# A head rearranged: modulation weights by blocks of rows, one block's statistics on ScalarE, fills moved between engines

## The chip, the cores and the metric

The kernel runs on one core of a Trainium2 chip. The metric is the time of one execution on the device in microseconds (us); the numbers given are the median of the runs and their spread. The engines are named as in the profile: PE (TensorE, matrix products; PEld is its loading of weights), DVE (VectorE), ACT (ScalarE), POOL (GpSimd) and SP (SyncE, which here only issues DMAs). ACT issues some DMAs too.

## What is computed

One block with sliding-window attention and a token-mixing MLP, both conditioned by a vector c. S = 2048 tokens, D = 512, 32 heads of 16, window 256, F = 1792; all inputs bfloat16.

```python
mod = silu(c) @ w_mod                      # 6 rows of 512: sa, ca, ga, sb, cb, gb
h = layernorm(x) * (1 + ca) + sa
x = x + ga * attention(h, wqkv, wo)        # causal, keys at most 255 back
h = layernorm(x) * (1 + cb) + sb
u = gelu(einsum('bsd,sf->bdf', layernorm(h), w1) + b1)
x = x + gb * (einsum('bdf,fs->bds', u, w2) + b2).transpose(0, 2, 1)
```

## The kernel before

All is one function. Tokens are cut into 16 blocks of 128 rows (`xres[0]` to `xres[15]`), four blocks make a group, and the features into four chunks of 128 (`dc`). The work has four parts: a head written out by hand (lines 626 to 735), attention over 16 steps (a step is one group of tokens and eight heads), the products with w1, and the products with w2 with the output.

**The head** brings the first group to the first scores. It builds the seeds of the masks (DVE fills, POOL selects), computes silu(c) as `sT` (exp on ACT, `sig` plus one on POOL, reciprocal and product on DVE), the statistics of blocks 0 to 3 (DVE's bn_stats and bn_aggr into `mv1[0]`), from them 1/sqrt(var + eps) as `r1` (POOL adds eps, POOL takes the power -0.5), the normalised blocks `xn1` (DVE), their transposes in PSUM (`pts`, PE), and the shift and scale of the 512 features as columns (`ps_fm`, by PE products of `wmod` with `sT`, one column each). DVE adds 0 or 1 to these (`plus_mod`) into `modFM`, and DVE and ACT write the scaled and shifted transposes to `h1T[0]`, two chunks each. PE then makes the first K and Q (line 720), DVE copies Q twice with alternate heads masked (`QP`, line 727), ACT copies K (`KT`), and the first scores can start. `warm(n)` puts in n filler products of zeros on PE.

For the columns, `fm(b)` takes chunks 2b and 2b + 1 for shift and scale and sums over the four row blocks of `wmod` at once; so it needs all rows of 256 columns, and the weights come in four DMAs of 256 columns and all rows, in runs of 512 bytes. `fm(0)` and `modFM[0]` serve the first two chunks before the transposes of blocks 2 and 3, `fm(1)` the others after them.

V is kept in `Vring[0]` to `Vring[2]`, one for each of three groups, with a column block of ones for each pair of heads, which gives the softmax's sums. The ones are written by ACT in the head (`ones_of`, two operations for each ring place). Zero halves of small copies of V (`VL`, `VU`) are filled by DVE (`zeros_of`), one of them, `VU[1]`, by POOL (line 712).

**What sets the order.** Each engine works off its own instructions in the order in which they were issued; they wait for one another by semaphores. In the head that is the order of the code. From the first scores on a planner (class `Order`) sets it: it takes tasks with an engine, an estimated cost, dependences and a rank, runs a small model of the engines' times and emits the tasks in that order. The ranks come from formulas plus a table, `PLACES`, and `BY` names the engines. The planner does not see the head, and its costs are fixed numbers. In attention ACT takes exp of the scores (line 868, two for each unit of scores) and PE makes scores and products with V; DVE turns the products (`turn`), POOL merges them (`merge`, line 912) and writes `QP` for later steps (line 1048); DVE normalises and transposes the next group (`n1ve`, `n1ng`, `h1T` at line 1155).

SP issues nearly all DMAs in the head in the order of the code: x blocks 0, 1, 3, the four parts of `wmod`, parts of `wqkv`, x blocks 4 to 7; ACT issues c and x block 2. Eight semaphores take turns, so an issue can wait for the landing of the one eight before.

## Time and profile before

| | us |
|---|---|
| median of 3 runs (lowest, highest) | 242.83 (242.56, 243.07) |
| profiled execution | 242.64 |
| its span, first to last instruction | 240.9 |
| PE busy | 234.5 |
| DVE busy | 177.3 |
| ACT busy | 162.1 |
| POOL busy | 96.1 |

The profiled execution is one of its own, and its time is 0.19 us under the median. Rows in order of time have the start in us from the span's start, the length in us, engine, line, operation, what it writes and reads with shapes, and how often (xN: N in a row, with one length for all); square brackets give idle time of the engine ahead of the row and what ended it. Matmul lengths include the pipeline, so neighbouring rows overlap. A row of a tile gives shortest/median/longest in ns. DMA rows give the time from issue to landing.

### The profile page before, as it was taken

To read this page: it belongs to the slowest core of one execution; us is meant where nothing else is said; L and a number is where in the kernel's file an instruction comes from. 1 tells how busy PE (TensorE), PEld (TensorE's weight loads), DVE (VectorE), ACT (ScalarE), POOL (GpSimd) and SP (SyncE) were. 2 spreads that over 40 slices of the span, in tenths; PEclk is the share of its full clock that TensorE was granted. 3 is DMA by queue.
4 is the path that set the end of the run, shared out by engine and by line. 5 is a ranking of instruction groups with operands and counts; after the bars stand their busy time and mean duration, and the time that the engine had idled before them with its cause. 6 is when DMAs were issued, how large, how long until landed. Compare 5 with 4: busy or idle time off the path is not lost.

```text
span 240.9 us, 9884 instructions
## 1 busy us (share of the span) xinstructions
PE 234.5 (97%) x4358; PEld 118.7 (49%) x4358; DVE 177.3 (74%) x421; ACT 162.1 (67%) x188; POOL 96.1 (40%) x149
## 2 busy tenths in 40 slices
PE   7999999999999999999999999999999999999994
PEld 2545555545655554554454455454444444444443
DVE  8799998878999899999356867989964306060644
ACT  7589999999999999999999999900446400000000
POOL 5319775741655466996310113686920000000000
PEclk9999999999999999999999999999999999999999
DMA  5998714063160343210110110069999001111031
GB/s 161 303 345 245 224 32 123 21 169 68 58 181 5 74 113 91 64 35 7 33 38 14 26 38 3 3 199 393 413 405 407 18 0 46 44 44 44 24 111 44
DMA packets 26151, 28.09 MB, mean 117 GB/s; under 512 B 10488, under 2 KB 23292, under 8 KB 26108
## 3 DMA queue, kind: packets, MB, share of 16 engines
q1 hardware_dynamic: 25956, 27.33, 36.0%
q8 instruction: 34, 0.56, 1.0%
q10 hardware_dynamic: 152, 0.13, 0.2%
q14 instruction: 9, 0.07, 0.1%
HBM read 22.55 MB, written 2.10 MB: 102 GB/s over the span
## 4 chain that ended last, share of the span: by engine, by line
PE 74%; DVE 19%; POOL 2%; issue 2%; ACT 2%; DVEq 0%; ACTq 0%; POOLq 0%
PE bk L606 18%; PE pss L1451 15%; PE bk L890 7%; PE pss L606 6%; PE bk L610 6%; PE pss L847 6%; DVE stats L599 5%; PE bk L1451 5%; PE bk L624 3%; DVE x L1255 2%; DVE t L899 2%; PE pss L859 2%; PE pss L819 2%; PE pss L828 1%; DVE QR L740 1%
## 5 line engine op out<-in xcount | busy, mean ns | idle before, releaser
L868 ACT ACTIVATE et<-pss 128x1024 bf16<-128x1024 f32 x152 | 141.7, 1050 | 1.5 <-PE pss L859 1.3
L1451 PEld LDWEIGHTS <-w2r 128*128 128x128 bf16 x238 | 23.1, 98 | 25.5
L912 POOL TENSOR_TENSOR merge<-t,zr 128x512 bf16<-128x512 f32 x16 | 16.9, 1058 | 32.3 <-DVE zr L908 32.2
L1460 DVE SCALAR_TENSOR_TENSOR o<-pss,bFM,bc_gb 128x512 bf16<-128x512 f32 (+2 forms) x13 | 8.8, 705 | 27.9 <-PE pss L1451 27.9
L1451 PE MATMUL pss<-guT,w2r 128*128 128x512 bf16 (+2 forms) x130 | 28.4, 363 | 0.0
L899 DVE STREAM_TRANSPOSE t<-bk 128x512 f32<-128x512 f32 x32 | 22.6, 706 | 7.2 <-PE bk L890 7.0
L847 PE MATMUL pss<-QP,KT 32*128 32x64 bf16 (+2 forms) x672 | 24.2, 236 | 0.7 <-DVE QP L727 0.3
L606 PE MATMUL bk<-h1T,wqkv 128*128 128x512 bf16 x80 | 21.0, 381 | 0.0
L1048 POOL TENSOR_SCALAR QP<-QR,mask_par 128x512 bf16<-128x512 bf16 x22 | 15.1, 694 | 14.8 <-PE pss L859 9.7
L606 PE MATMUL bk<-hb,w1a 128*128 128x512 bf16 x82 | 20.6, 380 | 0.2 <-DVE t L899 0.2
L606 PE MATMUL pss<-hb,w1b 128*128 128x512 bf16 x80 | 20.1, 379 | 0.1
L847 PEld LDWEIGHTS <-KT 32*128 32x128 bf16 x672 | 11.2, 92 | 17.7 <-issue 15.1
L890 PE MATMUL bk<-et,V 128*32 128x256 bf16 (+2 forms) x704 | 19.0, 240 | 0.7 <-DVE t L899 0.4
L599 DVE BATCH_NORM_STATS2 stats<-x 128x6 f32<-128x512 bf16 x28 | 18.8, 673 | 0.2
L890 PEld LDWEIGHTS <-V 128*32 128x32 bf16 x704 | 15.2, 97 | 7.2 <-issue 2.7
L606 PEld LDWEIGHTS <-w1b 128*128 128x128 bf16 x112 | 10.9, 98 | 13.7 <-issue 0.5
L859 PE MATMUL pss<-mask_q,mask_k 32*128 32x256 bf16 x240 | 17.5, 268 | 0.0
L606 PE MATMUL bk<-wod,OT 128*128 128x512 bf16 x54 | 13.9, 381 | 0.0
L606 PEld LDWEIGHTS <-w1a 128*128 128x128 bf16 x90 | 7.9, 98 | 10.3 <-issue 2.5
L606 PE MATMUL bk<-wqkv,h1T 128*128 128x512 bf16 x47 | 12.8, 381 | 0.0
L1255 DVE TENSOR_TENSOR x<-bk,x 128x512 bf16<-128x512 f32 x16 | 10.8, 674 | 2.8 <-PE bk L606 2.8
L921 DVE STREAM_TRANSPOSE OT<-merge 128x512 bf16<-128x512 bf16 x16 | 11.2, 700 | 2.0 <-POOL merge L912 1.8
(145 smaller groups left out, 396.5 us busy)
## 6 DMA issues: line engine op xcount, KB each, us to landing
w2r<-in_B_w_dram SPq DMA_DIRECT2D x14, 512.0 KB, 10.6
w1a<-in_B_w_dram SPq DMA_DIRECT2D x16, 224.0 KB, 3.7
w1b<-in_B_w_dram SPq DMA_DIRECT2D x8, 448.0 KB, 6.7
wmod<-in_w_mod_dram SPq DMA_DIRECT2D x4, 512.0 KB, 6.9
x<-in_A_x_dram SPq DMA_DIRECT2D x15, 128.0 KB, 5.4
out_dram<-otile SPq DMA_DIRECT2D x15, 128.0 KB, 1.8
VL<-V SPq DMA_DIRECT2D x15, 96.0 KB, 2.3
wmod<-in_w_mod_dram SPq DMA_DIRECT2D x4, 256.0 KB, 4.3
```

Of the source, the lines that this page charges most:

```text
L599: nc.vector.bn_stats(out=stats[:], in_=src)
L606: nc.tensor.matmul(out[:], lhsT=lhsT, rhs=rhs, start=start, stop=stop, skip_group_check=True)
L610: nc.tensor.matmul(out[cols, :], lhsT=lhsT[:, cols], rhs=rhs, start=start, stop=stop, tile_position=(0, 32 * j), skip_group_check=True,)
L847: mm(pss[j // 2][:, j % 2, c0 : c0 + nq], lhsT=keys(4 * tg + kb)[rows[j], :], rhs=QP[s][rows[j], par, q0 : q0 + nq], start=n == 0, stop=False,
L859: mm(o, lhsT=mask_k[rows[j], 0:P], rhs=rhs, start=False, stop=True, tile_position=(32 * j, 0), skip_group_check=True,)
L868: nc.scalar.activation(out=et[:], in_=held.pop(("pss", u, a))[:], func=ACT.Exp, scale=SCORE_SCALE)
L890: nc.tensor.matmul(po[32 * j : 32 * j + 32, q0 : q0 + nq], lhsT=v(j), rhs=held["et", s, k, j // 2][:, j % 2, c0 : c0 + nq], start=n == 0, ...
L899: nc.vector.transpose(out=held["t2", s][:, par, :], in_=psum.pop(("po", s, par))[:])
L912: nc.gpsimd.tensor_tensor(out=m[:].rearrange("p (b a d) -> p a b d", a=2, d=DH), in0=t2v(s, 0, DH, DH), in1=held["zr", s][:].to_broadcast( ...
L1048: engine[by(f"Qp{s}.{par}", "POOL")].tensor_scalar(out=QP[s][:, par, :], in0=QR[s][:], scalar1=mask_par[:, par : par + 1], scalar2=0.0, op ...
L1255: nc.vector.tensor_tensor(out=xres[tb][:], in0=pa[:], in1=xres[tb][:], op=ALU.add)
L1451: nc.tensor.matmul(py[:, lo:hi], lhsT=w2r[:, fc, tb * P : (tb + 1) * P], rhs=guT[fc][:, lo:hi], start=fc == made[0], stop=fc == made[-1], ...
```

## The change

*Weights by rows.* The shift and scale weights come in four DMAs of one row block each (128 rows, 1024 columns, runs of 2 KB); the first is issued by ACT, the others by SP. `fm(k)` now adds row block k to all eight columns, in one PSUM tile and one `modFM` of eight columns; its four calls are interleaved with the transposes, which now go block by block.

*Statistics.* Those of block 2 are made by ACT: the mean as an accumulated sum, a small step for its negative, and the variance as an accumulated square; both throw their wide output into `h1T[0]`, which is written for good later. DVE does blocks 0, 1 and 3, and adds eps for both pairs. POOL keeps the two powers, and its copy of `sT` (`sT_rep`) moves ahead of them.

*Fills.* ACT's fills of ones shrink from six to three and move behind the masks. Half of `Vring[1]` goes to DVE ahead of `modFM`. `Vring[2]` is filled by POOL behind the merge of step 0, in attention, in a task whose planned cost stays as it was. `VU[1]` goes from POOL to DVE. All selects of POOL come in one piece. The fillers on PE go from eleven to six ahead of the mask rows, with two ahead of `fm(0)` and two behind `fm(3)` instead of one, two and one.

*Ranks.* Two terms of -1e4 for steps done by ACT are dropped; the order of the rows that follow the head is otherwise unchanged on each engine, apart from the new fill on POOL.

DVE in the head before, from block 1's aggregate to the last of the four normalised blocks (x_64 to x_67 are blocks 0 to 3):

```order
L646 BN_AGGR mv_0_230<-stats 128x2
L643 BN_STATS stats<-x_66 128x6
L645 RECIPROCAL sig<-sig 128x4
L646 BN_AGGR mv_0_230<-stats 128x2
L648 TENSOR_TENSOR sT<-pss,sig 128x4
L643 BN_STATS stats<-x_67 128x6
L646 BN_AGGR mv_0_230<-stats 128x2
L683 TENSOR_SCALAR xn_332<-x_64,mv_0_230,r_293 128x512
L683 TENSOR_SCALAR xn_338<-x_65,mv_0_230,r_293 128x512
L534 MEMSET VU_214 64x384
L683 TENSOR_SCALAR xn_363<-x_66,mv_0_230,r_307 128x512
L683 TENSOR_SCALAR xn_369<-x_67,mv_0_230,r_307 128x512
```

The same place in the changed kernel (r_ve is variance plus eps):

```order
L598 BN_AGGR mv_0_229<-stats 128x2
L652 TENSOR_SCALAR r_ve<-mv_0_229 128x2
L666 RECIPROCAL sig<-sig 128x4
L667 TENSOR_TENSOR sT<-pss,sig 128x4
L597 BN_STATS stats<-x_67 128x6
L598 BN_AGGR mv_0_229<-stats 128x2
L652 TENSOR_SCALAR r_ve<-mv_0_229 128x2
L532 MEMSET VU_213 64x384
L699 TENSOR_SCALAR xn_335<-x_64,mv_0_229,r_298 128x512
L699 TENSOR_SCALAR xn_341<-x_65,mv_0_229,r_298 128x512
L699 TENSOR_SCALAR xn_355<-x_66,mv_0_229,r_305 128x512
L699 TENSOR_SCALAR xn_369<-x_67,mv_0_229,r_305 128x512
```

Block 2's statistics are gone, two small additions have come in, and the fill of VU stands ahead of all four normalised blocks. POOL in the head, before, from `sig` to the copy of `sT`:

```order
L634 TENSOR_SCALAR sig<-sig 128x4
L487 AFFINE_SELECT seed_182<-seed_182 16x64
L553 TENSOR_SCALAR r_ve<-mv_0_230 128x2
L555 TENSOR_TENSOR r_293<-r_ve,mhalf 128x2
L487 AFFINE_SELECT seed_181<-seed_181 16x64
L487 AFFINE_SELECT seed_182<-seed_182 16x64
L553 TENSOR_SCALAR r_ve<-mv_0_230 128x2
L555 TENSOR_TENSOR r_307<-r_ve,mhalf 128x2
L712 MEMSET VU_215 64x768
L746 COPY sT_rep<-sT 128x128
```

And now:

```order
L632 TENSOR_SCALAR sig<-sig 128x4
L485 AFFINE_SELECT seed_181<-seed_181 16x64
L485 AFFINE_SELECT seed_180<-seed_180 16x64
L485 AFFINE_SELECT seed_181<-seed_181 16x64
L668 COPY sT_rep<-sT 128x128
L659 TENSOR_TENSOR r_298<-r_ve,mhalf 128x2
L659 TENSOR_TENSOR r_305<-r_ve,mhalf 128x2
```

Both additions and the fill are gone, and the copy has moved ahead of the first power. POOL in attention around the merge of step 0, before:

```order
L1048 TENSOR_SCALAR QP<-QR,mask_par 128x512 x2
L912 TENSOR_TENSOR merge<-t_729,zr 128x2x16x16
L1048 TENSOR_SCALAR QP<-QR,mask_par 128x512 x2
L582 TENSOR_TENSOR n1r<-n1ve,mhalf 128x4
L584 TENSOR_TENSOR n1sh<-n1ng,n1r 128x4
```

And now:

```order
L1068 TENSOR_SCALAR QP<-QR,mask_par 128x512 x2
L927 TENSOR_TENSOR merge<-t_720,zr 128x2x16x16
L937 MEMSET V 128x64x16
L1068 TENSOR_SCALAR QP<-QR,mask_par 128x512 x2
L580 TENSOR_TENSOR n1r<-n1ve,mhalf 128x4
L582 TENSOR_TENSOR n1sh<-n1ng,n1r 128x4
```

The fill stands between the merge and the two QP of step 2. The diff, cut to its core:

```diff
-    for b in range(2):
-        for v in range(2):
-            cols = slice(v * D + 2 * P * b, v * D + 2 * P * b + 2 * P)
-            dma.dma_start(out=wmod[:, :, cols], in_=w_mod_v[:, :, cols])
+    for k in range(ND):
+        (dma if k else nc.scalar).dma_start(out=wmod[:, k, 0 : 2 * D], in_=w_mod_v[:, k, 0 : 2 * D])
...
-        run_selects(1)
+        run_selects(3)
...
-        for n in range(3):
-            ones_of(n)
...
+        def stats_by_act(tl):
+            neg = small.tile([P, 1], DT.float32, name="neg")
+            junk, mean = h1T[0][:, 0, :], mv[:, tl, 0:1]
+            nc.scalar.activation(out=junk, in_=xres[tl][:], func=ACT.Identity, scale=1.0 / D, accum_out=mean)
+            nc.scalar.activation(out=neg[:], in_=mean, func=ACT.Copy, scale=-root)
+            nc.scalar.activation(
+                out=junk, in_=xres[tl][:], func=ACT.Square, scale=root, bias=neg[:], accum_out=mv[:, tl, 1:2]
+            )
...
+        stats_by_act(2)
+        for tl in (0, 1, 3):
+            stats_of(xres[tl][:], mv[:, tl, :])
+            if tl == 1:
+                ve[0] = eps_of(0)
+                nc.vector.reciprocal(out=sig[:], in_=sig[:])
+                nc.vector.tensor_tensor(out=sT[:], in0=cT[:], in1=sig[:], op=ALU.mult)
+                nc.gpsimd.tensor_copy(out=sT_rep[:], in_=sT[:].unsqueeze(2).to_broadcast([P, ND, 32]))
+                power(0)
+        ve[1] = eps_of(1)
+        power(1)
+        zeros_of(0, True)
+        warm(6)
-        warm(11)
...
+        ones_of(0)
+        ones_of(1, 1)
...
+        warm(2)
+        fm(0)
+        turn_x(0)
+        turn_x(1)
+        fm(1)
+        turn_x(2)
+        fm(2)
+        turn_x(3)
+        fm(3)
+        warm(2)
+        nc.vector.memset(Vring[1][:, 2:4, :, DH : 2 * DH], 1.0)
+        nc.vector.tensor_tensor(out=modFM[:], in0=ps_fm[:], in1=plus_mod[:], op=ALU.add)
...
-        nc.gpsimd.memset(VU[1][0:64, :, :, :], 0.0)
+        zeros_of(1, True)
...
+        def more_ones(s):
+            merge(s)
+            if s == 0:
+                nc.gpsimd.memset(Vring[2][:, :, :, DH : 2 * DH], 1.0)
...
-                f"merge{s}", "POOL", 1.035, lambda s=s: merge(s), port=True, deps=[f"recip{s}"], take=[("m", s)],
+                f"merge{s}", "POOL", 1.035, lambda s=s: more_ones(s), port=True, deps=[f"recip{s}"], take=[("m", s)],
...
-                rank=rank + BEHIND["p2"] - (1e4 if first_eng == "ACT" else 0.0),
+                rank=rank + BEHIND["p2"],
```

## Prediction

> **What bounds the kernel now.** I read the page's span and chain first, then busy time by stage, then the first 13 us in order of time on DVE, POOL, PE and ACT, then the stretch from 26 to 32 us, where the only edit outside the head sits. Page, then stages (columns: stretch, PE, PEld, DVE, ACT, POOL busy us, clock, DMA share, GB/s):

> ```profile
> span 240.9 us, 9884 instructions
> PE 74%; DVE 19%; POOL 2%; issue 2%; ACT 2%; DVEq 0%; ACTq 0%; POOLq 0%
> ...
> 20.00:31.00 11.00, 10.34 (x289) 6.11 (x291) 10.79 (x25) 11.00 (x14) 9.06 (x14) 1.00 0.65 196
> ...
> 40.00:145.00 105.00, 104.16 (x2892) 54.97 (x2893) 88.27 (x183) 104.80 (x114) 51.80 (x63) 1.00 0.25 64
> ```

> The chain runs mostly over PE, but in attention ACT too is busy without a break: 11.00 of 11 us and 104.80 of 105. So the attention stage ends when the first exp starts, plus ACT's fixed work, plus what ACT idles. Two things can move the end: the start of the first exp, and new idle time in front of a later one. The head in order of time (start, length, engine, line):

> ```profile
> 3.78 0.26 POOL L634 TENSOR_SCALAR sig<-sig 128x4 f32<-128x4 f32 x1
> 4.65 0.18 DVE L646 BATCH_NORM_AGGREGATE mv<-stats 128x2 f32<-128x6 f32 x1
> 5.33 0.16 DVE L645 RECIPROCAL sig<-sig 128x4 f32<-128x4 f32 x1
> 5.67 0.68 DVE L643 BATCH_NORM_STATS2 stats<-x 128x6 f32<-128x512 bf16 x1
> 6.39 0.18 DVE L646 BATCH_NORM_AGGREGATE mv<-stats 128x2 f32<-128x6 f32 x1
> 6.50 0.70 DVE L683 TENSOR_SCALAR xn<-x,mv,r 128x512 bf16<-128x512 bf16 x2
> 6.67 0.30 POOL L553 TENSOR_SCALAR r_ve<-mv 128x2 f32<-128x2 f32 x1 [0.28 <-DVE mv L646]
> 7.05 0.72 POOL L555 TENSOR_TENSOR r<-r_ve,mhalf 128x2 f32<-128x2 f32 x1
> 7.22 0.38 DVE L534 MEMSET VU<- 64x384 uint32 x1
> 7.72 0.73 POOL L712 MEMSET VU<- 64x768 bf16 x1
> 7.80 1.12 DVE L683 TENSOR_SCALAR xn<-x,mv,r 128x512 bf16<-128x512 bf16 x2 [0.21 <-POOL r L555]
> 8.99 0.61 PE L688 MATMUL pss<-identity,xn 128*128 128x128 bf16 x8
> 9.43 0.54 PE L671 MATMUL bk<-sT,wmod 128*128 128x1 bf16 x16
> 9.63 1.45 ACT L706 ACTIVATE h1T<-pss,modFM 128x512 bf16<-128x512 bf16 x2 [1.16 <-PE pss L688]
> 10.04 0.15 DVE L701 TENSOR_TENSOR modFM<-bk,plus_mod 128x4 f32<-128x4 f32 x1
> 10.23 0.55 DVE L702 TENSOR_SCALAR h1T<-pss,modFM 128x512 bf16<-128x512 bf16 x1
> 10.69 0.34 DVE L510 TENSOR_REDUCE mask_par<-identity 128x1 f32<-128x64 bf16 x2
> 11.16 0.38 DVE L534 MEMSET VL<- 64x384 uint32 x1
> 11.84 1.14 DVE L727 TENSOR_SCALAR QP<-bk,mask_par 128x384 bf16<-128x384 f32 x2 [0.30 <-PE bk L720]
> 13.05 3.78 ACT L868 ACTIVATE et<-pss 128x1024 bf16<-128x1024 f32 x4 [0.88 <-PE pss L859]
> ```

> Read backwards: the first exp (13.05) waits for scores, these for QP (11.84), QP for the first products, these for the fourth piece of h1T, which ACT ends at 9.63 + 1.45 = 11.08. ACT waited for the transposes, and they for the last xn (7.80 + 1.12 = 8.92), which came after four statistics on DVE and an add and a power on POOL. The wait before 7.80 names POOL's r.

> **The change, part by part.** *Statistics and epsilon.* Block 2's statistics leave DVE, and POOL's add of epsilon becomes a DVE operation. DVE's series from the end of block 1's aggregate (4.65 + 0.18 = 4.83): epsilon 4.86, reciprocal 4.93, sT 5.12 (it needs the reciprocal, 0.16), block 3's statistics 5.20 to 5.88 (0.68), aggregate to 6.10, second epsilon 6.13 to 6.29, the fill of VU 6.20 to 6.58. The reciprocal comes 0.4 us sooner than at 5.33; sig is ready at 4.04. ACT now issues one weight DMA before its table load, which delays sig by an issue, about 0.5 us (rows below), to 4.54 at most: still ahead.

> POOL: the sT copy now stands ahead of the first power. sT ends at 5.28, the copy about 0.33 later at 5.69 (my estimate from the 0.30 of the small POOL row at 6.67), first power to 6.42, second 6.42 to 7.15. Before, the second ended at 7.77. The first is later than before, but VU's fill holds DVE until 6.58 anyway. A power does not hold DVE: VU's fill at 7.22 took 0.38 inside one, as the fill at 11.16 did beside nothing.

> *xn.* Now four in a row: two from 6.55 to 7.25 (0.70 a pair), two from 7.22 to 7.92. Before, the second pair took 1.12, since POOL filled half of VU beside it:

> ```profile
> L683 DVE TENSOR_SCALAR xn<-x,mv,r x4: 378/399/800, 6.5 to 8.5; 128x512 bf16<-128x512 bf16 x4
> ```

> One of the four took 800 ns instead of some 380. That fill moves to DVE, so 0.42 us goes. The last xn ends at 7.92 instead of 8.92: 1.00 us sooner.

> *Scale and shift.* Part of this is given back. Before, half of modFM was ready early and ACT started with the transposes; now one modFM stands behind all 32 weight products. After the last xn: four transposes start from 7.99, 0.056 apart (8 in 0.61, one lasts 0.22), then eight products 0.025 apart with a tail of 0.16 (16 in 0.54): end 8.61. modFM 8.68 to 8.83; ACT's two pieces 8.91 to 10.36 (1.45) instead of 11.08. So 0.72 of the 1.00 is left. From ACT's end to QP it was 11.84 - 11.08 = 0.76: QP at 11.12. DVE must be there too: two h1T from 8.87, 0.46 apart, masks at 9.79, fills of VL 10.26 and VU about 10.64 to 11.02. It just fits (0.10 spare). The fill of V ahead of modFM lies in the 0.7 us in which DVE waits for PE.

> *Statistics on ACT.* Three operations, none seen with an accumulated sum. Nearest rows: a 512-wide fill below, the 1024-wide exp of the 13.05 row above (four in 3.78, 0.95 each).

> ```profile
> 1.38 0.36 ACTq L436 DMA_DIRECT2D x<-in_A_x_dram  x1
> ...
> x<-in_A_x_dram ACTq DMA_DIRECT2D x1, 128.0 KB, 2.6
> ...
> L539 ACT ACTIVATE V<-zero 128x512 bf16<-128x512 bf16 x6 | 3.2, 617 | 0.0
> ```

> Block 2 lands at 1.38 + 2.6 = 3.98. At 0.62 for each wide one and some 0.4 for the one-column step between them with its waits it ends near 5.7, ahead of the second epsilon (6.13). I take that, since the size is the fill's. At 0.95 each, with waits of 0.6, it ends near 6.5 and pushes the second power by 0.4; sooner than the epsilon it gains nothing. Behind it stand four small mask copies (estimate by size: 1 us) and three fills of ones (3.2 / 6 each, 1.6 us), to 8.3, before h1T at 8.91.

> *Wider packets.* Issues and landings of the four weight loads:

> ```profile
> 2.18 2.09 SPq L440 DMA_DIRECT2D wmod<-in_w_mod_dram  x4
> ...
> DMA to landing us min/median/max: 4.1/4.3/4.5
> ```

> The last was issued near 3.75 and landed near 8.3; its products started at 9.43. Nothing waited for it, so wider packets alone are worth nothing here. They only must not be late: SP's third issue falls near 3.2, with 4.5 it lands at 7.7, needed at 8.2; at half a microsecond more it would cost that excess.

> *The fill in attention.* POOL fills Vring[2] behind the first merge.

> ```profile
> 26.10 1.06 POOL L912 TENSOR_TENSOR merge<-t,zr 128x512 bf16<-128x512 f32 x1 [1.11 <-DVE zr L908]
> 27.62 1.36 POOL L1048 TENSOR_SCALAR QP<-QR,mask_par 128x512 bf16<-128x512 bf16 x2 [0.46 <-DVE QR L740]
> ...
> 28.41 0.60 DVE L575 TENSOR_SCALAR n1ng<-n1mv 128x4 f32<-128x4 f32 x1
> 28.91 0.98 DVE L1155 TENSOR_SCALAR h1T<-bk,modFM 128x512 bf16<-128x512 bf16 x2
> ...
> 29.09 0.40 PE L837 MATMUL pss<-QP,KT 32*128 32x512 bf16 x4
> 29.95 1.05 PE L610 MATMUL bk<-wqkv,h1T 128*32 128x512 bf16 x16 [0.35 <-DVE h1T L1155]
> ...
> 25.86 5.77 ACT L868 ACTIVATE et<-pss 128x1024 bf16<-128x1024 f32 x6
> 32.03 1.02 ACT L868 ACTIVATE et<-pss 128x1024 bf16<-128x1024 f32 x1 [0.40 <-PE pss L859]
> ```

> Its 1024 elements at the 730 ns for 768 of the POOL fill above make 0.97 us, starting at 27.16. The gap there is 0.46, so the QP pair goes from 27.62 to 28.13 (+0.51) and the scores that need it from 29.09 to 29.60. PE has 0.35 us of waiting right behind them and ACT 0.40 before 32.03, so about 0.16 is left. If the fill packs its elements (half the price) the gap covers it: 0. If it takes 1.35 (twice a QP of 512), the pair is 0.87 late and 0.5 is lost. I take 0.15, by the only POOL fill in the trace of its size.

> Two edits cost nothing: the ranks of the LayerNorm steps on ACT leave every engine's row order there as it was, and the wider plus_mod fill is one small fill near 1 us, ahead of any need.

> **Sum.** -0.72 + 0.15 = -0.57 us. The profiled execution took 242.64 (span 240.9); its start and end outside the span don't change, so 242.07 there, and against the median of the runs, 242.83, 242.26. A measurement tells about 0.2%, 0.49 us, from no change; -0.57 is just beyond it.

> [...] DVE's 28.41 row took 0.60 for four elements: it ended when POOL's second QP did (28.98). With both QPs 0.51 later, the two tiny DVE operations meet them at another phase. If both slip between the two QPs, h1T stays at 28.91; if the second waits for the later QP, h1T goes to 29.4 and PE's wait at 29.95 grows by 0.5.
> [...]

> **Rivals.** (1) *The fill eats the gain*: h1T 0.5 later as above, or the fill at 1.35; -0.72 + 0.5 gives 242.6, no change. For it: the 28.41 row. Against: the same row's neighbour slipped through. (2) *The head gains little*: ACT's sums at the upper price, or the last weights late by 0.4; -0.72 + 0.4 + 0.15 gives 242.66, no change. For it: ACT's accumulation is unseen. Against: 0.2 us spare at the likely price. (3) *Slower: PE is still at its slow rate when the first products come.* Five filler products go from the start, and PE's rate rises only after a stretch of work:

> ```profile
> 2.33 4.85 PE L624 MATMUL bk<-zero 128*128 128x512 bf16 x11
> ...
> 8.15 0.59 PE L624 MATMUL bk<-zero 128*128 128x512 bf16 x2
> ```

> Eleven in 4.85 are 0.43 apart, two in 0.59 are 0.21 apart. Eight products of 384 columns at the slow 0.32 from 9.45 would end near 12.2 instead of 11.1, and the eight small ones behind them lose 0.4: together +1.5, net 243.7. It decides only if the slow rate lasts beyond about 11 us. Against: with fillers, mask rows and the first weights PE is still busy almost without a gap to 6.5, and the trace turned fast by 8.15.
> [...]

> **How the numbers follow.** Forecast 0.57 (own range 241.95 to 242.55: the head 0.55 to 0.85, the fill 0 to 0.2; some four fifths of it beyond the bound, one fifth inside). Fill eats the gain 0.20, all within 0.2%. Head gains little 0.11, within. Slow PE 0.12, nearly all slower. Faster 0.46, within 0.43, slower 0.11. The range goes from 241.95 to 243.0: it leaves out the slow PE's upper part and some of the lower tail.

> **What would show it.** Right: first QP near 11.1 and first exp near 12.35; four xn of 0.4 without a long one; the second power ending near 7.15; weights landed before PE reaches them; the POOL fill of about 1 us near 26.5, and ACT's idle before the exp at 32.03 larger by some 0.15 in all. Wrong: an epsilon that waits for ACT, filler products still 0.43 apart at 8 us, or PE waiting 0.8 us for h1T near 29.

## The result, and the profile after

| | before | after |
|---|---|---|
| median of the runs beside each other, us | 242.93 | 245.83 |
| lowest, highest (6 runs each) | 242.56, 243.39 | 244.91, 248.07 |
| ratio after / before, 95% interval | | 1.0131 [1.0085, 1.0177] |
| profiled execution, its span | 242.64, 240.9 | 245.19, 243.5 |

The change made the kernel slower by 2.9 us; the forecast was 0.57 faster, range 241.95 to 243.0. The page of after, span and busy times:

```profile
span 243.5 us, 9875 instructions
PE 235.1 (97%) x4353; PEld 119.0 (49%) x4353; DVE 176.8 (73%) x422; ACT 162.6 (67%) x190; POOL 95.9 (39%) x147
```

Busy times are those of before within 1 us (PE 234.5 there); what grew is idle time and slow time. Against before, the first exp starts 0.40 later (13.45 against 13.05), the exps from 26 us on 0.74, from 32 us 1.43, from 40 us 1.73, and the end comes 2.6 later. So the loss comes in steps, and only the first is in the head. The last lies behind attention, whose last exp is 1.6 late: near 165 us PE waits 0.8 us for the weights w1b to land, which it did not do before. The rows of the two pages, before and after (busy us, mean ns, then idle us ahead and what ended it):

```profile
L606 PE MATMUL pss<-hb,w1b 128*128 128x512 bf16 x80 | 20.1, 379 | 0.1
```

```profile
L604 PE MATMUL pss<-hb,w1b 128*128 128x512 bf16 x80 | 20.0, 380 | 0.8 <-DMA w1b<-in_B_w_dram 0.8
```

The head of after in order of time, PE:

```profile
2.50 2.74 PE L622 MATMUL bk<-zero 128*128 128x512 bf16 x6
5.18 0.71 PE L676 MATMUL bk<-seed,spread 16*128 16x320 bf16 x2
5.82 1.03 PE L622 MATMUL bk<-zero 128*128 128x512 bf16 x2
...
8.77 0.40 PE L691 MATMUL pss<-sT,wmod 128*128 128x1 bf16 x8
9.03 0.59 PE L704 MATMUL pss<-identity,xn 128*128 128x128 bf16 x4
9.41 0.40 PE L691 MATMUL pss<-sT,wmod 128*128 128x1 bf16 x8
9.67 1.01 PE L622 MATMUL bk<-zero 128*128 128x512 bf16 x2
```

The last two fillers start 0.38 apart: PE is still at its slow rate at 9.67, where before had two in 0.59 (0.21 apart) at 8.15. The trace's record of the granted clock has the full rate from 7.02 us on in before and from 10.56 on in after. DVE, POOL and ACT of after in the head:

```profile
5.74 0.19 ACT L644 ACTIVATION_READ_ACCUMULATOR h1T<-x,neg 128x1 f32 x1
6.48 0.17 DVE L652 TENSOR_SCALAR r_ve<-mv 128x2 f32<-128x2 f32 x1
6.73 1.13 POOL L659 TENSOR_TENSOR r<-r_ve,mhalf 128x2 f32<-128x2 f32 x1 [0.29 <-DVE r_ve L652]
6.97 0.54 DVE L699 TENSOR_SCALAR xn<-x,mv,r 128x512 bf16<-128x512 bf16 x2
7.90 0.74 DVE L699 TENSOR_SCALAR xn<-x,mv,r 128x512 bf16<-128x512 bf16 x2 [0.39 <-POOL r L659]
9.85 0.17 DVE L719 TENSOR_TENSOR modFM<-pss,plus_mod 128x8 f32<-128x8 f32 x1 [0.67 <-PE pss L691]
12.24 1.14 DVE L745 TENSOR_SCALAR QP<-bk,mask_par 128x384 bf16<-128x384 f32 x2
13.45 1.02 ACT L883 ACTIVATE et<-pss 128x1024 bf16<-128x1024 f32 x1 [0.89 <-PE pss L874]
```

The last xn ends at 8.64, 0.28 sooner than before, but modFM starts at 9.85 and the first QP at 12.24, 0.40 later than before. In attention, PE of after, and the exp behind it on ACT:

```profile
26.10 0.25 PE L834 MATMUL pss<-QP,KT 32*64 32x128 bf16 x4 [0.18 <-issue]
...
32.57 0.27 PE L905 MATMUL bk<-et,VL 128*32 128x64 bf16 x12 [0.90 <-issue]
...
33.46 1.02 ACT L883 ACTIVATE et<-pss 128x1024 bf16<-128x1024 f32 x1 [1.08 <-PE pss L874]
```

At 26.10 and 32.57 PE stops inside a series of products and waits for nothing that the profile shows ("issue"). The exp behind the second stop waits 1.08 where before it waited 0.40 (at 32.03). The place of these stops has a pattern. The page of after lists a queue of instruction packets, q8, with 34 of them and 0.56 MB, so 16 KB each. A row of PE is one product or one load of weights; there are 8706 of them (4353 each), 256 for each packet. Counted in order of start, the two stops come at rows 702 and 958, exactly 256 apart, and PE goes on 1.3 us (26.10) and 1.4 us (32.57) after a packet of this queue has landed (24.81, 31.13). Of the 33 packets behind the first, 31 start between 0.9 us ahead of and 4.0 us behind PE's arrival at row 446, 702, 958 and so on. So I read them as PE's program, which comes in pieces of 256 rows while it runs, with borders at rows 190, 446, 702, 958 and so on (an estimate from these counts). The changed kernel has five fillers less, ten rows, so each border lies ten rows later in the work. Two theories came from this: *the clock* (with five fillers less PE stays slow, or falls back) and *the code pieces* (a piece's packet waits in the load burst of 23 to 30 us, and PE arrives first). The third was that the moved fills and loads carry the loss by themselves. (Times of the clock and of packets are given from the span's start here; the expectations on record count both from 0.31 us before it.)

### The profile page after: what moved, and what is told of

It reads as the page before. It is cut to its first block, busy times and chain, and to the rows that moved or that the text cites. A ratio compares the mean times of both kernels' runs of the same rounds, so it can differ in the third digit from the quotient of the medians.

```text
span 243.5 us, 9875 instructions
## 1 busy us (share of the span) xinstructions
PE 235.1 (97%) x4353; PEld 119.0 (49%) x4353; DVE 176.8 (73%) x422; ACT 162.6 (67%) x190; POOL 95.9 (39%) x147
## 4 chain that ended last, share of the span: by engine, by line
PE 70%; DVE 17%; DMA 5%; issue 2%; POOL 2%; SPq 1%; ACT 1%; DVEq 0%; ACTq 0%
PE bk L604 18%; PE pss L1471 15%; PE bk L905 7%; PE pss L604 6%; PE pss L862 6%; PE bk L608 6%; PE bk L1471 5%; DVE stats L597 5%; DMA w1b<-in_B_w_dram 4%; PE pss L834 2%; PE pss L874 2%; DVE t L914 2%; DMA x<-in_A_x_dram 2%; PE pss L843 1%; DVE QR L758 1%
## 5 line engine op out<-in xcount | busy, mean ns | idle before, releaser
L927 POOL TENSOR_TENSOR merge<-t,zr 128x512 bf16<-128x512 f32 x16 | 16.9, 1056 | 32.6 <-DVE zr L923 32.5
L597 DVE BATCH_NORM_STATS2 stats<-x 128x6 f32<-128x512 bf16 x31 | 21.0, 677 | 0.5 <-DMA x<-in_A_x_dram 0.2
## 6 DMA issues: line engine op xcount, KB each, us to landing
x<-in_A_x_dram SPq DMA_DIRECT2D x15, 128.0 KB, 5.2
out_dram<-otile SPq DMA_DIRECT2D x15, 128.0 KB, 1.8
```

Of the source, the lines that this page charges most:

```text
L597: nc.vector.bn_stats(out=stats[:], in_=src)
L927: nc.gpsimd.tensor_tensor(out=m[:].rearrange("p (b a d) -> p a b d", a=2, d=DH), in0=t2v(s, 0, DH, DH), in1=held["zr", s][:].to_broadcast( ...
```

## The experiments

| kernel | median us (lowest, highest; runs) | ratio to before, 95% |
|---|---|---|
| e1: after, 11 fillers | 243.0 (242.61, 244.46; 12) | 1.0006 [0.9986, 1.0026] |
| e2: after, 6 and 5 tiny | 244.55 (242.16, 245.97; 9) | 1.0048 [1.0018, 1.0078] |
| e3: before, 6 fillers | 245.22 (244.24, 245.42; 6) | 1.0080 [1.0055, 1.0104] |
| e4: before, 6 and 5 tiny | 243.75 (242.64, 246.3; 12) | 1.0020 [1.0001, 1.0040] |
| e5: e1 with the head reordered | 242.95 (242.16, 247.88; 12) | 0.9991 [0.9972, 1.0010] |
| e6: e1, fill back on ACT | 243.85 (243.37, 244.66; 8) | 1.0036 [1.0020, 1.0052] |
| e7: e1, wod load later | 243.08 (242.52, 243.43; 12) | 0.9995 [0.9980, 1.0010] |
| e8: e1, two tiny on ACT | 243.68 (243.2, 244.76; 12) | 1.0030 [1.0015, 1.0045] |
| e9: after, wod load later | 245.24 (243.24, 246.71; 11) | 1.0079 [1.0047, 1.0111] |
| e10: e5, wod load later | 242.8 (242.25, 243.86; 12) | 0.9985 [0.9967, 1.0003] |
| e11: before, wod load later | 242.71 (242.6, 244.27; 12) | 0.9990 [0.9972, 1.0008] |
| e12: e8, wod load later | 243.17 (242.39, 243.75; 12) | 0.9996 [0.9978, 1.0014] |

The kernel before took 243.08 beside e1 to e4, 243.14 beside e5 to e8 and 242.88 beside e9 to e12. A filler has 512 columns and a tiny one four; the two tiny operations on ACT in e8 have one.

### e1 to e4: the fillers, their rows and their work

e1, and e2 in place of it; e3 and e4 are the same edits of before, whose call was `warm(11)`:

```diff
-        warm(6)
+        warm(11)                      # e1
+        warm(6)                       # e2
+        warm(5, cols=4)
```

> The changed kernel with eleven fillers on PE ahead of the mask rows again instead of six; all else as changed. Clock theory (six fillers leave PE's clock to come late or fall back): the clock is up near 7 to 8 us, the time returns to about 243 (242.3 to 243.8). Code theory (PE's instruction stream is ten rows shorter, so it reaches the ends of its 256-row pieces before the next piece is there, as at 26.1 and 32.6 us in the changed kernel): ten rows are back, so also about 243 to 243.8, with no stall at those rows. Third theory (the loss is made by the moved fills and loads): 245.5 or more as before this edit.

> The changed kernel with its six fillers and five more of only four columns behind them: ten rows more on PE, but next to no work. Clock theory: no help, 245 to 247, the clock up at 10 us or later or falling back. Code theory: about 243 to 244, no stall of PE inside a group of products near 26 and 32 us. Third theory: 245.5 or more.

> The kernel before with six fillers instead of eleven, nothing else: PE idles between about 5 and 6.5 us and its stream is ten rows shorter. Clock theory: 244 to 246, with the clock late in some executions. Code theory: 243.7 to 244.5, stalls of PE near 25 and 31 us. Third theory: 242.9, no change.

> The kernel before with six fillers and five of four columns: the rows are as many as before, only PE's work is less. Clock theory: 244 to 246 as with six alone. Code theory: 242.9, no change. Third theory: 242.9.

Five fillers put back take away the whole loss (245.83 to 243.0, the time of before), and five taken from before cost it 2.1 (243.08 to 245.22). So everything else in the change together is worth nothing that can be measured (the forecast gain of 0.57 would be a ratio of 0.9977, below e1's interval), and the theory of moved fills and loads falls. The five tiny products, which bring the rows back and hardly any work, recover about half: 1.28 in after, 1.47 in before. The clock shows in the stages of e2 (stretch, then PE, PEld, DVE, ACT, POOL busy, granted clock, DMA share, GB/s):

```profile
2.70:6.11 3.41, 3.41 (x14) 1.24 (x13) 2.69 (x9) 2.92 (x9) 2.45 (x11) 1.00 0.97 297
6.11:9.52 3.41, 2.25 (x47) 1.84 (x46) 2.82 (x9) 2.18 (x7) 1.47 (x2) 1.00 1.09 323
9.52:12.94 3.42, 3.37 (x19) 1.31 (x17) 2.19 (x8) 1.45 (x2) 0.00 (x0) 0.50 1.10 339
```

The record of the clock begins with its first rise, at 6.11 here (the column reads 1.00 ahead of it too, though the fillers there are 0.43 apart). PE then worked 2.25 of the next 3.41, and its rate fell back to half for one stretch, 9.52 to 12.94, just when the first products of Q and K came; the first exp started at 14.48. Within a run the changes of the clock lie a whole number of 3.41 us apart (e2: 6.11, 9.52, 12.94; after: 10.56 and 242.67, 68 of them); the expectations call this stretch the window. Its phase, and with it the first rise, differs from trace to trace: with the same eleven fillers the rise lies between 4.97 (e7) and 7.27 us (e6), and it came at 4.11 in e5.

How often the rate falls back is seen in the mean granted clock of each run: with six fillers in the second place (after, e2, e3, e4, e9) it is 0.984 to 0.993 in 22 of 44 runs, with ten or eleven (the other kernels and before in their company) in 1 of 183 (e5's 247.88). In e9 the seven such runs have a median of 245.44 and the other four 243.59; in e2 and e4 the difference is 0.95 and 0.53, and in after and e3 there is none that way. But this mean counts the time ahead of the first rise as full, so it misses a rate that comes late: e3's profiled run has a mean of 1.000, and its full rate came only at 12.67. In the three traces in which the slow rate met the first products of Q and K (e2, e3, e9), the first exp starts 1.42 to 1.54 later than in before. These products in before and in e3:

```profile
10.24 1.55 PE L720 MATMUL bk<-h1T,wqkv 128*128 128x384 bf16 x8
```

```profile
11.10 2.23 PE L720 MATMUL bk<-h1T,wqkv 128*128 128x384 bf16 x8
```

How many runs got the full rate late, and whether the tiny products change that number, is not shown.

### e5: the head's order

> The changed kernel with 17 fillers again, and the order in the head mended: fm(0) to fm(3) stand ahead of the transposes of blocks 2 and 3, ACT makes two fills ahead of the mask rows and one on either side of the copy of K, and DVE fills nothing ahead of modFM. Theory (PE's order, and not the normalised blocks, carried the head of the changed kernel with its fillers back, where modFM started at 9.81 and the first exp at 13.41): modFM near 8.5, first QP near 11.1, first exp near 12.3, so 1.1 us sooner; the time is 243.0 - 1.1 = 241.9, or up to 242.5 where PE, being sooner, meets more of its late code pieces (rows 702 and 958). Rival (the head is held by DVE or by weights of Q and K that have not landed): first exp at 13.2 or later and 242.9 to 243.2. Rival (the clock): the last four fillers come 1 us sooner, a window of 3.4 us falls thin, and products near 9.5 run at the slow rate: 244 or more in some runs.

```diff
+        ones_of(0)              # ahead of the mask rows
...
-        warm(2); fm(0); turn_x(0); turn_x(1); fm(1)
-        turn_x(2); fm(2); turn_x(3); fm(3); warm(2)
+        warm(1); fm(0); fm(1); turn_x(0); fm(2); turn_x(1); fm(3)
+        turn_x(2); turn_x(3); warm(4)
-        nc.vector.memset(Vring[1][:, 2:4, :, DH : 2 * DH], 1.0)
```

(There are ten fillers ahead of the mask rows; the two halves of `Vring[1]` are filled by ACT on either side of its copy of K.) DVE and ACT of e5:

```profile
8.44 0.17 DVE L717 TENSOR_TENSOR modFM<-pss,plus_mod 128x8 f32<-128x8 f32 x1
...
11.07 1.14 DVE L744 TENSOR_SCALAR QP<-bk,mask_par 128x384 bf16<-128x384 f32 x2
...
12.29 1.94 ACT L883 ACTIVATE et<-pss 128x1024 bf16<-128x1024 f32 x2 [0.37 <-PE pss L874]
```

These are the values that the forecast had for the changed kernel (QP 11.12, first exp 12.35). But this profile also had the full rate from 4.11 us, the earliest of all. Four profiles with the same 11 fillers and nearly the same head show what the phase alone does: the first exp starts at 12.51, 13.04, 13.41 and 13.47 where the full rate starts at 4.97 (e7), 6.15 (e8), 7.06 (e1) and 7.27 (e6), 0.42 us for each us. Carried on to 4.11 that line gives 12.15 (an estimate), sooner than e5's 12.29. So the theory's 1.1 us is not shown, and the median, 242.95 against 243.0, speaks for the rival.

### e6 and e8: the fill in attention, and ACT's own code pieces

> The changed kernel with 11 fillers, and its POOL fill of Vring[2] in attention taken back to two fills of ACT in the head, in the time in which ACT waits for the mask rows. Forecast's term (the fill costs 0.15, bounds 0 to 0.5): 243.0 - 0.15 = 242.85. Theory that the fill is free since n1ng slips ahead of the second QP: the same start of the exps near 32 us, to 0.1. ACT's code pieces (128 rows each, a border at row 62): two rows more move the border from between a semaphore wait and its exp, near 40 us, to between two exps, so the extra 0.3 at 39.6 goes: 242.7. If instead that 0.3 comes from what PE or DVE do there, it stays.

> The changed kernel with 11 fillers and two one-column operations more on ACT in the head, where it waits for the mask rows; they do no work. Theory (ACT's code comes in pieces of 128 rows; crossing a border costs 0.3 where it falls between a semaphore wait and its exp, and is hidden behind the exp in front where it falls between two exps): ACT's border moves by two rows, and the exp that started 1.23 after the one before it, near 40.2, starts 0.92 after it; 242.7. Rival (PE's scores or a buffer hold that exp): 1.23 stays, 243.0.

```diff
+        ones_of(2)              # e6, ahead of the mask rows
-            if s == 0:
-                nc.gpsimd.memset(Vring[2][:, :, :, DH : 2 * DH], 1.0)
...
+        for n in range(2):      # e8, at the same place
+            nc.scalar.activation(out=junk1[:], in_=zero[:, 0:1], func=ACT.Copy)
```

The exps that the forecast had in mind (32.03 in before) can't be compared between e6 and e1, because PE stops at row 958 ahead of them in both. Ahead of that stop the exps start alike, near 29 us at 29.10 without the fill (e6, head 0.06 later) and at 29.11 with it (e1). e7 below has the fill and no such stop, and there this exp, the first of the row below, waits 0.22, where in before it waited 0.40, so the fill costs nothing:

```profile
31.30 11.34 ACT L883 ACTIVATE et<-pss 128x1024 bf16<-128x1024 f32 x12 [0.22 <-PE pss L874]
```

The step of 0.3 near 40 us is ACT's: in all kernels made from after with 309 rows on ACT one exp starts late, right behind the event on which it waited, at ACT's row 63. ACT in e1, the exp at 40.21 and the two before it, and the same place in e8:

```profile
38.08 2.00 ACT L883 ACTIVATE et<-pss 128x1024 bf16<-128x1024 f32 x2
...
40.21 1.02 ACT L883 ACTIVATE et<-pss 128x1024 bf16<-128x1024 f32 x1
```

```profile
38.71 2.02 ACT L886 ACTIVATE et<-pss 128x1024 bf16<-128x1024 f32 x2
```

In e1 the second exp of the first row starts at 38.98 and the next 1.23 behind it; in e8, with two rows more on ACT, the two in the row start 0.92 apart, and so do those of e6. So that step hangs on the number of rows ahead of it, as a border between two pieces of ACT's program would have it. That a piece has 128 rows is an estimate (on the page of after the other instruction queue, q14, has 9 packets and 0.07 MB, so 8 KB each, half of the 16 KB that go with 256 rows of PE), since one border alone was seen. It is worth nothing at the end, though: in the median e6 is 0.85 and e8 0.68 slower than e1, not faster. Their profiles have longer stops at row 958 (0.74, 0.53, against 0.43 in e1) and waits for w1b near 165 to 170 us (0.35, 1.31), which e1's lacks; whether that is the doing of the edits or the spread of one execution stays open.

### e7, e9, e11, e12: the load burst

> The changed kernel with 11 fillers; the load of wod (512 KB), which SP issued near 23 us, is issued behind the V copies of the step after, near 34 us, still before its use at 41. Nothing else moves. Theory (PE's code pieces queue behind the load burst): the packet for row 958 lands near 29 instead of 30.5, PE does not stop at row 958 (0.53 before), and the exps from 33 us on come 0.4 to 0.5 sooner: 242.5. A stall at row 1214 or 1470 may take its place, 0.3 at most, since those had 1.7 spare. Rival (the stall is the wait for something else, data or a buffer): 0.53 stays at that row and the time is 243.0.

> The changed kernel as it is, with its six fillers, and the load of wod behind the V copies near 34 us. Theory (of the 2.9 that the change cost, about half is PE's code pieces that land too late behind the load burst, half the slow rate in the head): the idle time of PE at rows 702 and 958 (0.46 and 1.17 in the profile of the changed kernel) goes, the head stays as it is: 245.8 - 1.3 = 244.5, ratio near 1.006. Rival (the slow rate carries all, and those stalls are a mark of a late head): 245.8 as before, ratio 1.012. Rival (the pieces carry all): 243.0, ratio 1.000.

> The kernel before, with the load of wod later and nothing else. Theory: its rows 702 and 958 had 0.1 to 0.2 to spare in the one profile, so the later load gains little in the middle and cuts the upper runs: 242.9, ratio 0.998 to 1.000. If before's runs too lose 0.5 at a row in most executions, 242.6, ratio 0.997 or less.

> The changed kernel with 11 fillers, two one-column operations more on ACT, and the load of wod later: against the same without the two operations (243.08, ratio 0.9995 [0.998, 1.001]) it shows what ACT's border is worth where PE's pieces don't disturb. Theory: the exp near 40 starts 0.9 behind the one before, not 1.23, and all after it 0.3 sooner: 242.75, ratio near 0.998. Rival (ACT waits later for PE in any case, or the two operations delay the mask rows): 243.1 or more, ratio 0.9995 or more.

```diff
-        later("wo", wod[:], wo_v, 512, 12)
+        later("wo", wod[:], wo_v, 512, 12, ["back0"])
```

When the packet landed, and the stop: the time at the border in which PE started neither a product nor a load of weights (us, from the traces). The brackets in PE's rows are smaller, since they count from the end of the product before; the expectations on record put the same stops up to 0.1 higher (0.46, 1.17 and 0.53).

| kernel | row 702: landed, stop | row 958: landed, stop |
|---|---|---|
| before | 23.75, 0.02 | 29.42, 0.00 |
| after | 24.81, 0.40 | 31.13, 1.09 |
| e1 | 24.32, 0.11 | 30.19, 0.43 |
| e2 | 25.29, 0.00 | 31.10, 0.29 |
| e3 | 25.88, 0.41 | 30.97, 0.00 |
| e4 | 24.97, 0.23 | 30.31, 0.00 |
| e5 | 22.87, 0.00 | 28.99, 0.31 |
| e6 | 24.19, 0.00 | 30.76, 0.74 |
| e7 | 23.12, 0.00 | 27.70, 0.00 |
| e8 | 23.52, 0.00 | 29.73, 0.53 |
| e9 | 25.88, 0.46 | 29.78, 0.00 |
| e10 | 23.81, 0.13 | 27.87, 0.00 |
| e11 | 23.69, 0.08 | 28.52, 0.00 |
| e12 | 23.98, 0.00 | 28.13, 0.00 |

With 512 KB of load out of its way the packet for row 958 lands 0.9 to 2.5 us sooner (2.6 to 3.4 us after PE has passed row 702, instead of 4.1 to 5.0), and the stop is gone in all four pairs that had one (1.09 in after, 0.00 in e9; 0.43 in e1, 0.00 in e7; 0.53 in e8, 0.00 in e12; 0.31 in e5, 0.00 in e10): that stop goes with the late landing of its packet. Of the two stops expected of e3 only the first came. The one at 702 stays in e9; its packet ran from 24.81 to 25.88, beside the copies of V and the next load, 512 KB of `wmod` (issued at 24.16), and what made it late is not shown. The stop stands in PE's row

```profile
27.17 0.25 PE L834 MATMUL pss<-QP,KT 32*64 32x128 bf16 x4 [0.25 <-issue]
```

The times moved less than the stops. e9 gained 0.6 of the 1.3 expected (1.0079 against 1.0131, with intervals that overlap); seven of its eleven runs still lost a stretch of the clock. e7, e11 and e12 stayed where e1, before and e8 were within their intervals, only with fewer high runs (e7's highest is 243.43, e1's 244.46). Part was given back at row 1470, where the late load now stands before the packet: PE stopped there for 0.23 in e7, 0.17 in e11 and 0.34 in e12, and not in e1. In e12 that took most of the 0.3 which ACT's border gave.

### e10: what might beat both

> The changed kernel with 17 fillers, the head's order mended (products of the weights ahead of the last transposes, fills on ACT around the mask rows and the copy of K) and the load of wod later: the version that should beat both. Theory: the mended head gives 0.4 to 0.7 against the kernel before, the code pieces cost nothing, ACT's border falls between two exps: 242.4, ratio near 0.997. Rival (the head's gain is only the phase of the clock's window, as one profile with the full rate from 4.42 us suggests): 243.0 in the middle, ratio 0.9995.

It joins e5 and e7. The ratio, 0.9985 [0.9967, 1.0003], does not tell it from before, and the forecast of 0.997 is at the edge of the interval. Its profile shows what holds the head where PE does not (the full rate came at 4.57, the first exp at 12.90):

```profile
5.87 0.69 DVE L597 BATCH_NORM_STATS2 stats<-x 128x6 f32<-128x512 bf16 x1 [0.50 <-DMA x<-in_A_x_dram]
...
7.13 1.13 POOL L659 TENSOR_TENSOR r<-r_ve,mhalf 128x2 f32<-128x2 f32 x1 [0.69 <-DVE r_ve L652]
```

DVE, with one block less to do, waits for block 3 to land, and POOL idles until the second epsilon; the second power then takes 1.13 again.

## Why the prediction was wrong, point by point

*Fillers.* This is the step that failed. The change part costed the statistics, the xn, the fills, the weights and the ranks, and gave the five missing fillers no term at all; they came only as rival (3), with 0.12. The runs put them at 2.8 us in the changed kernel (e1) and 2.1 in before (e3). A part of that is what the rival said (PE at the slow rate when the first products come), and its price of 1.5 is what the traces that show it have (1.42 to 1.54 at the first exp in e2, e3 and e9). The chance was wrong: "against" stood that PE is busy almost to 6.5 and that the trace turned fast by 8.15. The one trace shown had one phase, with the full rate from 7.02. In four profiles with six fillers the full rate came at 6.11 (e2), 6.24 (e9), 10.56 (after) and 12.67 (e3), and 22 of 44 such runs lost a stretch after the first rise. I also thought only of the rate coming late, as in e3; it can come, find PE working 2.25 of 3.41, and go again, as in e2.

The profiled run of after shows neither at its first exp, which starts 0.04 after e1's. Its span is 1.7 longer than e1's, and this stands at rows 702 and 958 (0.3 and 0.5 at the exps) and behind the last exp (0.9, most of it the wait for w1b).

*Ten rows.* No step spoke of the instruction packets. In the trace of before PE reached rows 702 and 958 1.53 and 1.62 us after their packets landed, 0.2 more than at the stops of after (1.29 and 1.43); e8 stopped at row 958 until 1.64 after the landing, so that margin is not firm. How the 2.8 us of the five fillers divide stays open: the rows recovered 1.3 to 1.5 with tiny fillers in their place (e2, e4), 0.6 by the later load (e9, intervals that overlap). Nor did a step look behind the last exp. PE's products wait for w1b for 0.7 to 1.2 us in the three profiles with five fillers less (after, e3, e9) and not in those of before, e1, e2 and e4; but e8 waits 1.3 with all its fillers, so the cause of this wait is not shown.

*Statistics and epsilon.* Nearly as said on ACT: the sums end at 5.93, forecast near 5.7, and nobody waits for them; each accumulated sum adds a read of 0.19. The second epsilon came at 6.48, not 6.13. The second power took 1.13 instead of 0.73 and ended at 7.86, not 7.15. That a power does not hold DVE is true of this one: two xn (0.22 and 0.39, the first from 6.97) run inside it, from 6.73 to 7.86. They do not explain its length either. In e1, e5, e6, e7 and e8 the same two xn start 0.24 behind it, and it takes 0.81 to 0.82; in after, e2, e9, e10 and e12 it takes 1.12 to 1.13. What differs between the two groups is POOL's idle time ahead of it, 0.10 in the first and 0.29 or more in the second; why that should cost 0.3 is not shown. Both powers of e1:

```profile
5.71 1.66 POOL L659 TENSOR_TENSOR r<-r_ve,mhalf 128x2 f32<-128x2 f32 x2
```

*xn.* The long xn of 800 ns is gone, as forecast: e1, whose power ended sooner, has

```profile
6.79 1.35 DVE L699 TENSOR_SCALAR xn<-x,mv,r 128x512 bf16<-128x512 bf16 x4
```

four in 1.35, the last ending at 8.14 (forecast 7.92, before 8.92).

*Scale and shift.* The term "-0.72" was mis-sized even without the clock. In e1, whose full rate came at 7.06 as in before (7.02), the last xn is 0.78 sooner and modFM still starts at 9.81 (forecast 8.68), the first exp at 13.41, 0.36 later than before. I had put the products right behind the last xn; but in the code they stand behind two fillers, the mask rows and the transposes of each block, and PE works through without a gap (e1):

```profile
7.12 0.44 PE L676 MATMUL bk<-seed,spread 16*128 16x320 bf16 x2
7.50 0.60 PE L622 MATMUL bk<-zero 128*128 128x512 bf16 x2
7.94 0.34 PE L691 MATMUL pss<-sT,wmod 128*128 128x1 bf16 x8
```

So PE's order sets the pace of the head, and the work taken from DVE was not what PE waited for. No phase of the clock that was seen gives the new head a lead over the old: e11, whose head is that of before, has its first exp at 12.81 with the full rate from 5.70, and the four profiles in the section on e5 give 12.82 for that rate (an estimate from their line).

*Wider packets.* Nothing, as forecast. *Fill in attention.* The operation's size was right (0.97 forecast), and the QP pair moved behind it:

```profile
27.49 0.95 POOL L937 MEMSET V<- 128x1024 bf16 x1
28.43 1.40 POOL L1068 TENSOR_SCALAR QP<-QR,mask_par 128x512 bf16<-128x512 bf16 x2
```

but its cost was 0, not 0.15: ACT's idle time ahead of the exp in question is 0.22 in e7, where it was 0.40 in before, and rival (1) did not come. *ACT's ranks*: nothing, as forecast.

## What to carry to other kernels

That a filler product computes nothing does not make it free to remove: five of them were worth 2.8 and 2.1 us here (e1, e3). Count what such a product does for the clock at every phase, and from one trace take the phase as one draw (first rise at 4.97 to 7.27 with the same eleven). When instructions are added or dropped ahead of a tight stage, look for idle time put down to "issue" at equal distances in rows (here rows 702 and 958, 0.40 and 1.09 us in after, with ten rows less ahead of them), and see which loads run while the packet for such a row is due: without 512 KB of them it landed 0.9 to 2.5 us sooner. Before taking work from one engine, see whether the next link has its own queue behind it: here PE's order, not the engine relieved, set the start.
